# Halves of W3's row blocks between w_out's blocks, six accumulators, and another order of loads and first steps

## The chip, the cores and the metric

The kernel runs on one core of a Trainium2 chip. The metric is the device time of one execution in microseconds, the median of several runs.

## The reference

Two layers follow each other. The first is a decayed linear recurrence over q, k, v of shape 4 x 8 x 768 x 64, with one decay per head; the second is a gated product with weights:

```python
gamma = 1.0 - 2.0 ** (-5.0 - np.arange(H))
for t in range(S):
    state = gamma[None, :, None, None] * state + np.einsum('bhd,bhe->bhde', k[:, :, t], v[:, :, t])
    y[:, :, t] = scale * np.einsum('bhd,bhde->bhe', q[:, :, t], state)
x = y.transpose(0, 2, 1, 3).reshape(B * S, H * D)      # 3072 x 512
a = x @ w1                                             # w1, w2: 512 x 1024
b = x @ w2
h = a * b @ w3                                         # w3: 1024 x 1024
out = h @ w_out                                        # w_out: 1024 x 512
```

Inputs and output are float32.

## The kernel before

The products run in float16 with float32 sums. `h @ w_out` is folded ahead: the kernel computes W3O = W3 @ w_out once, as eight row blocks `W3O[f]` of 128 x 512, so that each step needs only three products: with W1, with W2 and with W3O.

The recurrence is worked in chunks of 128 rows. A step of the second layer takes 256 rows (two batches, one chunk), and there are 12 of them. The first 256 rows of batches 0 and 1 are steps 0 and 1 and are worked by the class `Pairs` (`b0` for batch 0, `b1` for batch 1); later steps by `scores`, `intra`, `kv`, `inter` and `outputs_back`. For a `Pairs` object the sequence is: cast q, k and v to float16 (`q_cast`, `k_cast`; `v_cast` multiplies by decays), transpose q and k on TensorE (PE) and copy the transposes out of PSUM, `scores` (q times k) and two masking products on VectorE (DVE) called `am_back`, twice; `intra` (scores times v), twice; `kv` and `state` (the state after 128 rows); `inter` (q times that state); `outputs_back`, twice, which scales the result on DVE into the tile `XT` that the second layer reads. `next_state_add` (DVE) and `next_state_decay` (GpSimd, POOL) prepare the state for the chunk after.

The schedule is written by hand: each engine executes its instructions in the order of the code, and the code orders PE, DVE, ScalarE (ACT), POOL and the load queue on SyncE (SP) by where each call stands. Buffers are rotated in pools. Every load goes through `dma_in`, on SP, into a stage tile of 512 KB (`new_stage`), of which there are 22; the first 22 loads need no free buffer, later ones wait until an earlier tile has been cast.

The order of loads before: W3 rows 0 to 3 alternate with the four blocks of w_out, then W3 rows 4 to 7, then q, k, v of batch 0, q, k, v of batch 1, W1 (4 tiles), W2 (4 tiles), then q, k, v of later steps. W3 and w_out have rows of 4 KB per partition; q and k, v of the first steps come in pieces of 512 bytes.

W3O is built like this. `cast_w3(f)` casts a row block to float16 (DVE and ACT, half each, for f < 4; whole on one of them after). `w3_transpose(f)` transposes it by eight PE instructions into PSUM, and DVE copies it out. `w3_part(f, i)` adds two matmuls with w_out's block i to the accumulator of f. Blocks 0 to 3 have an accumulator in PSUM each and are worked as w_out's blocks come; blocks 4 to 7 follow one at a time through `W3Block`. `busy(m)` issues m matmuls of zeros that nothing reads. `cast_wo(i)` casts w_out's block i, half on ACT and half on POOL.

After that, step 0's first product is worked by rows of W1: `by_rows(W1, ps, d)` issues eight matmuls with W1's tile d into four PSUM banks, so that it can start before all of W1 has landed. Batch 1's `scores`, `intra`, `kv` and `inter` stand between these rows. Then come `f1.a_unit(f)`, step 1's products with W1 (four matmuls each, which read all of XT[1]), then `by_rows(W2, ps, d)` between further `a_unit`s, and from there the regular steps. The tail of the W1 part (lines 818 to 825) reads:

```python
    by_rows(W1, ps, 2)
    nc.gpsimd.tensor_copy(W2[0][:, :], w2_st[0][:, :])
    nc.gpsimd.tensor_copy(W2[1][:, :], w2_st[1][:, :])
    by_rows(W1, ps, 3)
    for i in range(4):
        cast_to(pa[i], ps[i], i > 1)
    for f, tag in ((0, "X0"), (1, "Y1"), (2, "Y0"), (3, "X1")):
        f1.a_unit(f, tag)
```

In the profile PE's products with a step's x are psF (lines 636 and 795) or psG (the first `a_unit`s), psO is the product with W3O, psW the products of W3 with w_out, psA `scores`, psY `intra` and `inter`, psK `kv`.

Of the kernel before, what the change touches and what calls it, by code (L numbers as in the profile page):

```python
# [9 lines left out]
FP = mybir.dt.float32  # L10
# [8 lines left out]
def kernel(  # L19
# [51 lines left out]
    def load_q(n):  # L71

        g, e = divmod(n, 2)
        if g >= NSTEP // 2:
            return
        bp, cp = divmod(g, NCH // 2)
        q_in[n] = load_pairs(q, bp * 2 + e, cp)

    def load_pairs(src, b, cp):
        t = new_stage()  # L80
        dma_in(
            t[:, :].rearrange("p (h x) -> p h x", x=2 * D),
            src[b, :, cp * 2 * C : (cp + 1) * 2 * C, :].rearrange("h (p t) d -> p h (t d)", t=2),
        )
        return t
# [19 lines left out]
    def new_stage():  # L105
        return wstage.tile([128, 1024], FP, tag="wst", name="stg")

    def load_rows(src, i):
        t = new_stage()
        dma_in(t[:, :], src[i * 128 : (i + 1) * 128, :])  # L110
        return t

    def load_wo(i):
        t = new_stage()
        dma_in(
            t[:, :].rearrange("p (t n) -> p t n", t=2),
            moe_w_out[i * 256 : (i + 1) * 256, :].rearrange("(p t) n -> p t n", t=2),
        )
        return t

    w3_st, wo_st = [], []
    for i in range(4):
        w3_st.append(load_rows(moe_w3, i))
        wo_st.append(load_wo(i))
    for f in range(4, 8):
        w3_st.append(load_rows(moe_w3, f))
    for e in range(2):
        load_q(e)
        k_in[e] = load_pairs(k, e, 0)
        v_in[e] = load_pairs(v, e, 0)  # L130
    w1_st = [load_rows(moe_w1, d) for d in range(4)]
    w2_st = [load_rows(moe_w2, d) for d in range(4)]
    load_q(2)
    load_q(3)
# [35 lines left out]
    keep = const.tile([128, L], FP, name="keep")  # L170
    keep_t = const.tile([128, 2, 128], FP, name="keep_t")

    def masks_and_decays():

        nc.gpsimd.memset(keep[:, :], 1.0)
        for s in range(2):
            r = slice(s * L, (s + 1) * L)
            nc.gpsimd.affine_select(
                out=keep[r, :], in_=keep[r, :], compare_op=mybir.AluOpType.is_ge, fill=0.0,
                base=0, pattern=[[1, 2], [2, 32]], channel_multiplier=-1,  # L180
            )

        nc.gpsimd.memset(keep_t[:, :, :], 1.0)
        for s in range(2):
            for t in range(2):
                nc.gpsimd.affine_select(
                    out=keep_t[half(s), t, :], in_=keep_t[half(s), t, :], compare_op=mybir.AluOpType.is_ge,
                    fill=0.0, base=-t, pattern=[[1, 2], [2, 64]], channel_multiplier=-2,
                )
        for h in range(H):  # L190
            for s in range(2):
                nc.gpsimd.memset(LGP[half((h + s) % 2), s, h // 2 : h // 2 + 1], math.log(gam[h]))
        for h in range(H):
            p, r = h // 2, (h % 2) * 64
            nc.gpsimd.memset(GS[r : r + 64, p : p + 1], gam[h] ** C)
# [20 lines left out]
    def cast_to(dst, src, on_dve):  # L216
        if on_dve:
            nc.vector.tensor_copy(dst, src)
        else:
            nc.scalar.copy(dst, src)  # L220

    def cast_wo(i):
        dst = WO[i][:, :, :].rearrange("p a n -> p (a n)")
        nc.scalar.copy(dst[:, 0:512], wo_st[i][:, 0:512])  # L224
        nc.gpsimd.tensor_copy(dst[:, 512:1024], wo_st[i][:, 512:1024])  # L225

    def cast_w3(f):
        t = att.tile([128, 1024], HP, tag="qT", name="w3h", bufs=5)
        st = w3_st[f]
        if f < 4:  # L230
            nc.vector.tensor_copy(t[:, 0:512], st[:, 0:512])  # L231
            nc.scalar.copy(t[:, 512:1024], st[:, 512:1024])
        else:
            cast_to(t[:, :], st[:, :], f == 4)
        W3h[f] = t

    def bank(tag, shape, dtype, name):
        return ps_at.tile(shape, dtype, tag=tag, name=name)

    def w3_transpose(f):  # L240
        src, ps = W3h.pop(f), bank(("X0", "X1")[f % 2], [128, 1024], HP, "psW3")
        for g in range(8):
            c0 = (g // 2) * 256 + g % 2
            nc.tensor.transpose(  # L244
                ps[:, g * 128 : (g + 1) * 128], src[:, c0 : c0 + 255 : 2], ident16[:, :]
            )
        w3t[f] = att.tile([128, 1024], HP, tag="k16" if f < 3 else "v16", name="w3t", bufs=3)
        nc.vector.tensor_copy(w3t[f][:, :], ps[:, :])  # L248

    def w3_part(f, *parts):  # L250

        for i in parts:
            for r in range(2):
                g = i * 2 + r
                nc.tensor.matmul(  # L255
                    acc[f], lhsT=w3t[f][:, g * 128 : (g + 1) * 128], rhs=WO[i][:, r, :],
                    start=(g == 0), stop=(g == 7),
                )
            if i == 3:
                cast_to(W3O[f][:, :], acc[f], f < 3)  # L260

    class W3Block:
        def __init__(self, f):
# [413 lines left out]
    def cast_w(W, st, d, on_dve):  # L677
        cast_to(W[d][:, :], st[d][:, :], on_dve)

    def busy(m, tag="Y0", n=512):  # L680
        if tag:
            ps = bank(tag, [128, 512], FP, "psZ")
        else:
            ps = ps_f.tile([128, 512], FP, tag="psF", name="psZ")
        for _ in range(m):
            nc.tensor.matmul(ps[:, 0:n], lhsT=Z[:, 0:128], rhs=Z[:, 0:n], start=True, stop=True)  # L686

    cast_w3(0)
    busy(8)
    acc = [ps_f.tile([128, DM], FP, tag="psF", name="psW")[:, :] for _ in range(4)]  # L690
    w3_transpose(0)
    cast_wo(0)
    busy(2, n=400)
    w3_part(0, 0)
    busy(3)
    cast_w3(1)
    w3_transpose(1)
    busy(3)
    cast_wo(1)
    w3_part(0, 1)  # L700
    w3_part(1, 0, 1)
    cast_w3(2)
    w3_transpose(2)
    busy(2, n=400)
    cast_wo(2)
    w3_part(0, 2)
    w3_part(1, 2)
    w3_part(2, 0)
    cast_w3(3)
    w3_transpose(3)  # L710
    w3_part(2, 1, 2)
    cast_wo(3)
    masks_and_decays()
    cast_w3(4)
    for f in range(3):
        w3_part(f, 3)
    cast_w3(5)
    w3_part(3, 0, 1)
    w3_transpose(4)
    cast_w3(6)  # L720
    w3_part(3, 2, 3)
    w3_transpose(5)
    cast_w3(7)
    output_decays()
    wb = W3Block(4)
    wb.mm(4)
    w3_transpose(6)
    wb.mm(4)
    wb.back()
    q_cast(0, nc.gpsimd)  # L730
    wb = W3Block(5)
    wb.mm(4)
    w3_transpose(7)
    wb.mm(4)
    wb.back()
    b0, b1 = Pairs(0), Pairs(1)
    b0.k_cast(nc.vector)
    q_transposes(0, "Y0", False)
    b0.v_cast(nc.gpsimd, 0)
    b0.v_cast(nc.gpsimd, 1)  # L740
    wb = W3Block(6)
    wb.mm(4)
    b0.k_transposes("Y1", True)
    wb.mm(4)
    am_back = b0.scores(0)
    wb.back()
    am_back(0)
    am_back(1)
    wb = W3Block(7)
    wb.mm(3)  # L750
    am_back = b0.scores(1)
    am_back(0)
    b0.kv(True)
    b0.state()
    am_back(1)
    b0.intra(0)
    q_cast(1, nc.scalar, nc.gpsimd)
    wb.mm(1)
    q_transposes(1, "X0", False)
    b1.k_cast(nc.gpsimd)  # L760
    last = ended(b0.intra(1), nc.gpsimd)
    b0.outputs_back(0)
    wb.mm(1)
    b1.k_transposes(None, False, 2)
    b0.inter(last)
    b0.next_state_add()
    b0.outputs_back(1)
    b1.v_cast(nc.gpsimd, 0)
    nc.scalar.copy(W1[0][:, 0:512], w1_st[0][:, 0:512])  # L769
    nc.gpsimd.tensor_copy(W1[0][:, 512:1024], w1_st[0][:, 512:1024])  # L770
    b1.v_cast(nc.gpsimd, 1)
    wb.mm(1)
    am_back = b1.scores(0)
    am_back(0)
    am_back(1)
    wb.mm(2)
    wb.back()
    nc.scalar.copy(W1[1][:, 0:512], w1_st[1][:, 0:512])
    nc.gpsimd.tensor_copy(W1[1][:, 512:1024], w1_st[1][:, 512:1024])
    b0.next_state_decay()  # L780
    nc.gpsimd.tensor_copy(W1[2][:, :], w1_st[2][:, :])
    nc.scalar.copy(W1[3][:, 0:512], w1_st[3][:, 0:512])
    nc.gpsimd.tensor_copy(W1[3][:, 512:1024], w1_st[3][:, 512:1024])

    ffn = [Ffn(m) for m in range(NSTEP)]
    f0, f1 = ffn[0], ffn[1]
# [12 lines left out]

    pa = [hold[i // 2][:, i % 2 * 512 : i % 2 * 512 + 512].rearrange("p (a n) -> p a n", a=2) for i in range(4)]  # L800
    ps = four_banks()
    by_rows(W1, ps, 0, (2, 3, 4, 5))
    am_back = b1.scores(1)
    am_back(0)
    am_back(1)
    b1.intra(0)
    by_rows(W1, ps, 0, (6, 7, 0, 1))
    by_rows(W1, ps, 1, range(4))
    b1.intra(1)
    b1.kv(False)  # L810
    b1.state()
    b1.outputs_back(0)
    by_rows(W1, ps, 1, range(4, 8))
    b1.inter()
    b1.outputs_back(1)
    b1.next_state_add()
    b1.next_state_decay()
    by_rows(W1, ps, 2)
    nc.gpsimd.tensor_copy(W2[0][:, :], w2_st[0][:, :])
    nc.gpsimd.tensor_copy(W2[1][:, :], w2_st[1][:, :])  # L820
    by_rows(W1, ps, 3)
    for i in range(4):
        cast_to(pa[i], ps[i], i > 1)
    for f, tag in ((0, "X0"), (1, "Y1"), (2, "Y0"), (3, "X1")):
# [153 lines left out]
```

## Time and profile before

| | |
|---|---|
| runs, us | 183.87, 183.89, 182.86; median 183.87 |
| profiled execution | 184.97 us, of which the span in the profile is 183.3 |
| granted TensorE clock | 1.0 |
| PE busy | 174.3 us, 95% of the span, 2634 matmuls |
| DVE, ACT, POOL busy | 108.7, 71.8 and 71.5 us |
| bytes moved by DMA | 39.71 MB, mean 217 GB/s |

PE means the matmuls and PEld the loads of their stationary operand, which lie beside them. Busy shares are means over the span. The profile gives three more things that matter here: slices of the span with a digit for each engine's busy share in tenths; the chain of work that ended last, followed back from the end; and for each load its issue on SP and the time from issue to landing.

### The profile page before, as it was taken

How to read it: one execution, taken by the hardware profiler on the slowest of the kernel's cores; microseconds unless marked ns; L12 is line 12 of the kernel's file. 1: busy time of each engine (PE TensorE's matmuls, PEld its weight loads, DVE VectorE, ACT ScalarE, POOL GpSimd, SP SyncE). 2: the span in 40 equal slices, each digit the busy share in tenths (PEclk: the TensorE clock that was granted, in tenths of full speed). 3: DMA queues.
4: the chain of work that ended last, by engine and by line, in shares of the span. 5: the costliest groups of instructions: out<-in, count | busy, mean ns of one | idle time of the engine just before them, and what ended most of it. 6: DMA issues, size and time to landing. Idle time of an engine off the chain costs nothing.

```text
span 183.3 us, 6222 instructions
## 1 busy us (share of the span) xinstructions
PE 174.3 (95%) x2634; PEld 124.7 (68%) x2634; DVE 108.7 (59%) x204; ACT 71.8 (39%) x157; POOL 71.5 (39%) x127
## 2 busy tenths in 40 slices
PE   7689999799999999999999999999999999999992
PEld 2345646588766696785876858758678587685871
DVE  2247658670769678648468484395685865845430
ACT  4353844455630332433333424334244242342531
POOL 3127526864547650824416364037450260000000
PEclk9999999999999999999999999999999999999999
DMA  5999999999999989999999999999999930200203
GB/s 215 344 418 404 299 273 288 368 401 278 215 260 234 174 254 221 221 283 223 213 212 175 322 192 239 207 191 290 225 149 250 159 114 7 114 0 29 89 0 114
DMA packets 79530, 39.71 MB, mean 217 GB/s; under 512 B 57360, under 2 KB 74000, under 8 KB 79504
## 3 DMA queue, kind: packets, MB, share of 16 engines
q1 hardware_dynamic: 79072, 38.81, 89.9%
q8 instruction: 20, 0.33, 0.8%
q10 hardware_dynamic: 432, 0.52, 0.8%
q14 instruction: 6, 0.05, 0.1%
HBM read 29.36 MB, written 6.29 MB: 195 GB/s over the span
## 4 chain that ended last, share of the span: by engine, by line
PE 78%; SPq 9%; DMA 9%; ACT 1%; issue 1%; ACTq 0%
PE psF L636 40%; PE psO L663 23%; SPq L63 9%; DMA stg<-in_moe_w_out_dram 5%; DMA stg<-in_moe_w_dram 4%; PE psF L795 4%; PE psY L531 2%; PE psY L599 2%; PE psA L383 2%; PE psG L636 2%; PE psK L551 1%; PE psTk L357 1%; ACT w L220 1%; PE psTq L328 0%; ACT osb L667 0%
## 5 line engine op out<-in xcount | busy, mean ns | idle before, releaser
L636 PE MATMUL psF<-xt,w 128*128 128x256 f16 x672 | 76.5, 273 | 0.0
L636 PEld LDWEIGHTS <-w 128*128 128x128 f16 x704 | 68.4, 98 | 10.3
L651 DVE TENSOR_TENSOR ht<-pa,psF 128x256 f16<-128x256 f32 x88 | 36.9, 420 | 37.6 <-PE psF L636 31.6
L663 PE MATMUL psO<-w3o,ht 128*128 128x512 f16 (+2 forms) x200 | 44.0, 371 | 0.3 <-issue 0.3
L645 ACT COPY pa<-psF 128x256 f32<-128x256 f32 x80 | 29.7, 371 | 37.1 <-PE psF L636 37.1
L663 PEld LDWEIGHTS <-ht 128*128 128x128 f16 x200 | 18.5, 98 | 19.9 <-issue 0.6
L667 ACT ACTIVATE osb<-psO 128x512 f32<-128x512 f32 (+2 forms) x25 | 14.5, 580 | 44.4 <-PE psO L663 44.4
L614 DVE TENSOR_TENSOR xt<-psY,YS 64x512 f16<-64x512 f32 (+1 forms) x29 | 21.1, 728 | 5.2 <-PE psY L599 4.8
L310 POOL TENSOR_TENSOR v<-stg,VS 128x512 f16<-128x512 f32 x20 | 20.6, 1042 | 5.1 <-DMA stg<-in_v_dram 5.0
L303 POOL CAST k<-stg 128x512 f16<-128x512 f32 x18 | 11.0, 612 | 25.3 <-DMA stg<-in_k_dram 25.1
L290 POOL CAST q<-stg 128x1024 f16<-128x1024 f32 (+1 forms) x12 | 12.0, 1003 | 15.3 <-DMA stg<-in_q_dram 10.8
L390 DVE TENSOR_TENSOR am<-psA,keep 128x512 f16<-128x512 f32 x20 | 12.8, 680 | 0.6 <-PE psA L383 0.6
L566 POOL TENSOR_TENSOR t<-s,GS 128x512 f16<-128x512 f32 x8 | 8.3, 1040 | 12.3 <-DVE s L565 12.3
L795 PE MATMUL psF<-xt,w 128*128 128x256 f16 x64 | 8.3, 273 | 1.1 <-ACT w L769 1.0
L255 PE MATMUL psW<-wo,w3t 128*128 128x512 f16 x32 | 7.7, 379 | 1.0 <-ACT wo L224 1.0
L269 PE MATMUL psW<-wo,w3t 128*128 128x512 f16 x32 | 8.6, 381 | 0.0
L248 DVE COPY w3t<-psW 128x1024 f16<-128x1024 f16 x8 | 5.5, 688 | 4.9 <-PE psW L244 4.9
L795 PEld LDWEIGHTS <-w 128*128 128x128 f16 x64 | 5.9, 98 | 2.7 <-ACT w L769 1.5
L686 PE MATMUL psZ<-zeros 128*128 128x512 f16 (+1 forms) x18 | 5.9, 461 | 1.3 <-DVE zeros L143 1.3
L244 PEld LDWEIGHTS <-w3h 128*128 128x128 f16 x64 | 4.1, 98 | 3.7 <-DVE w3h L231 2.3
L573 DVE TENSOR_TENSOR t<-psK,t 128x512 f16<-128x512 f32 x9 | 6.2, 690 | 0.6 <-PE psK L551 0.5
L225 POOL CAST wo<-stg 128x512 f16<-128x512 f32 x4 | 2.4, 612 | 10.2 <-DMA stg<-in_moe_w_out_dram 10.2
(92 smaller groups left out, 148.1 us busy)
## 6 DMA issues: line engine op xcount, KB each, us to landing
stg<-in_moe_w_dram SPq DMA_DIRECT2D x16, 512.0 KB, 9.3
stg<-in_q_dram SPq DMA_DIRECT2D x12, 512.0 KB, 6.3
out_dram<-osb SPq DMA_DIRECT2D x22, 256.0 KB, 3.5
stg<-in_k_dram SPq DMA_DIRECT2D x20, 256.0 KB, 5.7
stg<-in_v_dram SPq DMA_DIRECT2D x20, 256.0 KB, 5.8
stg<-in_moe_w_out_dram SPq DMA_DIRECT2D x4, 512.0 KB, 7.8
stg<-in_k_dram SPq DMA_DIRECT2D x2, 512.0 KB, 10.5
stg<-in_v_dram SPq DMA_DIRECT2D x2, 512.0 KB, 8.8
```

The lines of the kernel that those rows point to most:

```text
L63: nc.sync.dma_start(dst, src)
L290: (nc.scalar.copy if eng is nc.scalar else eng.tensor_copy)(dst[:, :].rearrange("i (t h d) -> i h t d", t=2, d=D)[:, hs, :, :], src[:, :]. ...
L303: (nc.scalar.copy if eng is nc.scalar else eng.tensor_copy)(dst, src)
L310: eng.tensor_tensor(v16[:, e, :].rearrange("j (h d) -> j h d", d=D), v32[:, e, :].rearrange("j (h d) -> j h d", d=D), VS[:, 2, :].unsqueez ...
L390: nc.vector.tensor_tensor(am[:, r, :, :], ps[r][:, :, :], keep[:, :].unsqueeze(1).broadcast_to((128, NP * 2, L)), MULT,)
L614: nc.vector.tensor_tensor(XT[m][to, :, s, :].rearrange("p (a e) (i t) -> p a e t i", e=2, t=2), psYs[m][s][fr, :, :].rearrange("p (a e) (t ...
L636: nc.tensor.matmul(ps[:, :], lhsT=W[d][:, f * 128 : (f + 1) * 128], rhs=self.x(d), start=(d == 0), stop=(d == 3),)
L645: nc.scalar.copy(self.pa[f][:, :], ps[:, :])
L651: nc.vector.tensor_tensor(self.HT[:, f, :], self.pa.pop(f)[:, :], ps[:, :], MULT)
L663: nc.tensor.matmul(psO[:, :], lhsT=self.HT[:, f, e * 128 : (e + 1) * 128], rhs=W3O[f][:, cs], start=(f == 0), stop=(f == 7),)
L667: nc.scalar.activation(osb[:, cs], psO[:, :], AF.Copy, scale=final_scale)
L795: nc.tensor.matmul(ps[f // 2][:, f % 2, :], lhsT=W[d][:, f * 128 : (f + 1) * 128], rhs=f0.x(d), start=(d == 0 and f % 2 == 0), stop=(d == ...
```

## The change

The loads come in another order. W3's row blocks 0 to 5 are loaded as two halves of 512 columns each (`load_w3(f, h)`, 128 rows of 2 KB), first halves first, between w_out's blocks; rows 6 and 7 stay whole. q, k and v of batch 0 stand between the last W3 loads. Two tiles of W1 come before q, k, v of batch 1 and two after.

W3 is worked in these halves: `cast_w3(f, h)` casts 512 columns on DVE, `w3_half(f, h)` transposes them by four PE instructions and DVE copies them out. Six row blocks have an accumulator each (`acc_of`): two in the banks Y0 and Y1, four in the psF pool. Rows 6 and 7 go through `W3Block` as before. The filler matmuls write into the accumulators ahead of their first product and are shorter. The masks and the decays on POOL are made in two functions at two places.

The first two steps are ordered anew: batch 0's work follows its loads between the last W3 blocks; all of `by_rows` row 0 and half of row 1 come before batch 1's transposes and scores, row 2 lies around `intra(0)`, row 3 before `inter`. Batch 1's k cast and its two copies of transposes move to DVE; W1 row 2 is cast by ACT alone.

```diff
+    for x in ((0, 0), "o0", (1, 0), (2, 0), (3, 0), "o1", (4, 0), (5, 0),
+              (0, 1), "o2", (1, 1), (2, 1), "o3", (3, 1)):
+        if x[0] == "o":
+            wo_st[int(x[1])] = load_wo(int(x[1]))
+        else:
+            load_w3(*x)
+    load_q(0)
+    load_w3(4, 1)
+    load_w3(5, 1)
+    k_in[0] = load_pairs(k, 0, 0)
+    w3_st[6] = load_rows(moe_w3, 6)
+    v_in[0] = load_pairs(v, 0, 0)
+    w3_st[7] = load_rows(moe_w3, 7)
+    w1_st = [load_rows(moe_w1, d) for d in range(2)]
+    load_q(1)
+    k_in[1] = load_pairs(k, 1, 0)
+    v_in[1] = load_pairs(v, 1, 0)
+    w1_st += [load_rows(moe_w1, d) for d in range(2, 4)]
...
+    def cast_w3(f, h):
+        W3h[f, h] = att.tile([128, 1024], HP, tag="qT", name="w3h", bufs=5)
+        nc.vector.tensor_copy(W3h[f, h][:, 0:512], w3_st[f][:, h * 512 : h * 512 + 512])
...
+    def w3_half(f, h):
+        src = W3h.pop((f, h))
+        ps = bank(("X0", "X1")[len(units) % 2], [128, 512], HP, "psW3")
+        units.append(f)
+        for g in range(4):
...
+        nc.vector.tensor_copy(w3t[f][:, h * 512 : h * 512 + 512], ps[:, :])
...
+    def acc_of(f):
+        if f not in acc:
+            acc[f] = bank(f"Y{f}", [128, DM], FP, "psW") if f < 2 else ps_f.tile([128, DM], FP, tag="psF", name="psW")
+        return acc[f]
...
+    b0.kv(True)
+    b0.state()
+    w3_transpose(7, "X0", False)
     last = ended(b0.intra(1), nc.gpsimd)
     b0.outputs_back(0)
+    wb = W3Block(7)
+    wb.mm(2)
     b0.inter(last)
     b0.next_state_add()
     b0.outputs_back(1)
...
+    cast_w1_halves(0, nc.scalar, nc.gpsimd)
+    cast_w1_halves(1, nc.scalar, nc.gpsimd)
+    wb.mm(6)
+    wb.back()
+    q_cast(1, nc.scalar, nc.gpsimd)
+    b1.k_cast(nc.vector)
     b1.v_cast(nc.gpsimd, 0)
     b1.v_cast(nc.gpsimd, 1)
...
-    by_rows(W1, ps, 0, (2, 3, 4, 5))
+    by_rows(W1, ps, 0)
+    by_rows(W1, ps, 1, range(4))
+    q_transposes(1, "X0", True)
+    by_rows(W1, ps, 1, range(4, 8))
+    b1.k_transposes("X1", True)
+    am_back = b1.scores(0)
+    am_back(0)
+    am_back(1)
     am_back = b1.scores(1)
     am_back(0)
     am_back(1)
+    b0.next_state_decay()
+    cast_w1_halves(2, nc.scalar, nc.scalar)
+    cast_w1_halves(3, nc.scalar, nc.gpsimd)
+    by_rows(W1, ps, 2, range(4))
     b1.intra(0)
-    by_rows(W1, ps, 0, (6, 7, 0, 1))
-    by_rows(W1, ps, 1, range(4))
+    by_rows(W1, ps, 2, range(4, 8))
     b1.intra(1)
     b1.kv(False)
     b1.state()
     b1.outputs_back(0)
-    by_rows(W1, ps, 1, range(4, 8))
+    by_rows(W1, ps, 3)
     b1.inter()
     b1.outputs_back(1)
     b1.next_state_add()
     b1.next_state_decay()
-    by_rows(W1, ps, 2)
     nc.gpsimd.tensor_copy(W2[0][:, :], w2_st[0][:, :])
     nc.gpsimd.tensor_copy(W2[1][:, :], w2_st[1][:, :])
-    by_rows(W1, ps, 3)
```

`cast_w1_halves(d, *engs)` casts the two halves of W1's tile d on the two engines named.

## The prediction

> **What bounds the kernel now.** I read the page's slices first, then the chain of waits in order of time, then stretches of the head, then POOL's and DVE's instructions there.
>
> ```profile
> PE   7689999799999999999999999999999999999992
> DMA  5999999999999989999999999999999930200203
> ...
> PE psF L636 40%; PE psO L663 23%; SPq L63 9%; DMA stg<-in_moe_w_out_dram 5%; DMA stg<-in_moe_w_dram 4%; PE psF L795 4%; PE psY L531 2%; PE psY L599 2%; PE psA L383 2%; PE psG L636 2%; PE psK L551 1%; PE psTk L357 1%; ACT w L220 1%; PE psTq L328 0%; ACT osb L667 0%
> ```
>
> A slice is 4.6 us. From the eighth on TensorE is full; the only stretch where it is not is the head, and there the transfers are full from the second slice. The chain says the same: queue and transfers carry it to 33.3 us, TensorE from then on.
>
> ```profile
> 25.98 7.30 DMA stg<-in_moe_w_dram
> 33.28 0.02 issue
> 33.31 0.63 ACT w L769
> 33.93 0.05 issue
> 33.98 0.61 PE psF L795 x4
> ...
> 37.52 0.39 PE psY L498 x8
> 37.91 1.85 PE psF L795 x16
> 39.76 1.75 PE psG L636 x16
> 41.51 0.87 PE psF L795 x8
> 42.38 0.45 PE psG L636 x4
> ...
> 43.23 0.95 ACT w L220
> 44.18 0.05 issue
> 44.23 1.05 PE psF L795 x8
> ```
>
> Columns: start, length, what. The first W1 row block lands at 33.28; 5.8 us of unbroken PE work follow; step 1's first unit, `f1.a_unit(0)` (psG), starts at 39.76. From there the work is the same in both kernels and PE waits only at 44.2, so **the start of that unit fixes the end of the kernel**. I call it U. In the stretch 34 to 39.5 us PE has no gap:
>
> ```profile
> 34.00:39.50 5.50, 5.50 (x120) 4.19 (x121) 3.27 (x6) 1.96 (x4) 4.08 (x6) 1.00 1.02 408
> ```
>
> (length; busy PE, PEld, DVE, ACT, POOL; clock; DMA share; GB/s.) Between `b1.inter` (L498, over at 37.9) and U lie 16 matmuls of `by_rows` rows 2 and 3, 1.85 us. They cover the second `outputs_back` on DVE, on which U waits, and the state's sum and decay:
>
> ```profile
> 37.36 1.34 DVE L509 TENSOR_TENSOR xt<-psY,YS 128x512 f16<-128x512 f32 x2
> 38.60 0.40 DVE L483 TENSOR_TENSOR s<-psK,t 128x256 f32<-128x256 f32 x1
> ...
> 39.09 0.61 POOL L490 TENSOR_TENSOR t<-s,GS 128x256 f16<-128x256 f32 x1 [1.18 <-DVE s L483]
> 39.64 1.04 POOL L819 CAST w<-stg 128x1024 f16<-128x1024 f32 x1
> ```
>
> XT[1] is ready at 38.70, a microsecond before its use, and the first W2 block is cast by 40.68, before its use at 41.51.
>
> [...] share 1.0 from 6.6 us on, so an order of loads moves landings against each other but not the last one. [...] packets of 4 KB took 159 ns in the median, of 2 KB (the stores) 84, of 512 B 27 to 31.
>
> **Landings, the clock of the head.** From each issue and its time to landing: W3 rows 0 to 3 and w_out at 4.1, 5.4, 7.9, 9.2, 10.6, 11.8, 13.1, 14.4; W3 row 4 at 15.7; q0 21.35, k0 24.2, v0 26.1, q1 27.8, k1 29.6, v1 31.25; W1 at 33.3, 34.6, 35.9 (worked out), 37.25. A 4 KB-row tile costs 1.29 us, a q/k/v tile 1.6 to 2.9. A load is issued once the load eight places before it has landed (ninth issue at 4.68 after a landing at 4.1); with halves the eight are smaller, but the smallest eight-load window holds 5 tiles, 6.4 us of transfer, so I take no starvation.
>
> **The change, part by part.**
>
> 1. *Halves.* 12 half loads in place of 6: 6 tiles move as 2 KB packets. 16 x 84 ns against 8 x 159 per tile and engine: +0.07 us each, **+0.43 us** for every landing behind them. Bounds: -1.2 (the 2.6 us that the third load took after the second, where 1.3 is the rule, doesn't recur) to +1.2 (a W1 tile behind a q/k/v tile took 2.03, not 1.29: +0.74 for more changes of kind).
> 2. *Order.* W1 rows 0 and 1 now come before q1, k1, v1; rows 2 and 3 after. 22 tiles lie up to the last W1 row in both, so W1 row 2 lands at 35.9 + 0.43 = 36.3 and row 3 at 37.7. But v1 has two more weight tiles ahead: 31.25 + 2 x 1.29 + 0.43 = **34.3**, k1 29.6 + 3.0 = 32.6. v0 gets one tile fewer: 25.25; W3 row 7 about 26.6 (before: 19.6).
> 3. *W3 work in halves.* The transposes (64) and products (64) stay; 12 copies of 512 columns replace 6 of 1024 (0.69 us). 18 filler matmuls (5.9 us busy) become 19 of 256 columns. All of it lies ahead of 26.6 us, under the loads: counted **nothing**. Without that cover each half would cost one more DVE cast and copy with its hand-over, 6 x 0.5 us. Masks and decays on POOL are divided, same instructions, under the same cover. SP issues six loads more, 0.44 us each; a half takes 0.64 us to transfer, so SP stays ahead of the transfers.
> 4. *Tail of W3 and b0.* Row 7: ACT cast 26.6 + 1.05 = 27.7; transposes wait for `b0.kv`, which needs both v casts (25.25 + 2 x 1.04 = 27.35): 27.75 to 28.4; ACT copy 1.01 to 29.5; two products, `inter`, six products (0.215 each) to 31.7; ACT's `W3O[7]` copy to 32.35. q1's ACT cast is queued behind it: 0.62 to 33.0, though q1 landed at 30.8. Meanwhile `by_rows` 0 and half of 1: PE at 33.1.
> 5. *Batch 1's scores.* q transposes to 33.55, DVE copy to 34.5, rest of row 1, k transposes, DVE copy to 35.4, `scores(0)` 0.4, then four mask products on DVE of 0.65 to **38.6**. Batch 1's k cast comes from POOL to DVE (0.69, from 32.6, before q's copy needs DVE) and both copies from ACT to DVE, which has nothing else between 33.3 and 34.
> 6. *Rows 2 and 3 after the scores.* W1 row 2 is cast at 36.3 + 0.65 = 37.0, scores end at 37.5; four matmuls 0.5, `intra(0)` 0.45, four 0.5: 38.95. The v casts that it reads end on POOL at 34.3 + 2.08 = 36.4; batch 0's decay (0.61, moved behind them) ends at 37.0, before W1 row 3 lands, whose second half is queued behind it. So `intra(1)` starts about 38.6 to 38.95 by either road; 0.55, `kv` 0.3, row 3 (landed and cast by 38.4) 0.9, `inter` 0.39: 40.8. On the cheaper readings (rows at 0.44 per four, no scores wait) 40.5. I take 40.7.
> 7. *The cover is gone.* Nothing follows `inter` now but U. `outputs_back(1)`, 0.67 + 0.1 for the hand-over, lies open: **U at 41.5, against 39.76: +1.75.** What is late next: the sum 0.40, decay 0.61 and W2 cast 1.04 follow on DVE and POOL, so W2 row 0 is ready at 43.5 while U's four units end at 43.25: **+0.3**. The ACT cast that PE waited for at 44.2 hangs on the fifth unit, which moves along, so nothing is recovered. W2 lands by 42.9, q2 by 44.7, before their uses.
>
> Sum: 1.75 + 0.3 = **+2.05 us**. It is made against the profiled execution, 184.97 with a span of 183.3; the shown median is 183.87, 1.1 below it. I put the sum on the median: **185.9 us**, +1.1%.
>
> **Rivals.**
> - *Loads earlier* (0.20). The early 1.3 us loss doesn't recur and the whole clock moves by up to -1.2 + 0.43: U at 40.7 or a little earlier, +0.5 to +1.4, 184.4 to 185.3. For: it is one gap in a regular series. Against: the engines were full in it (share 1.00), only the packets were slower.
> - *Loads later* (0.17). Mixed tiles cost 2.0 instead of 1.29 at three or more new changes of kind, or eight small loads fall behind: W1 row 2 at 37.5, U at 42.7, +3.2, 187.1. Speaks for it: share over 1.1 but 292 GB/s around 18 to 24 us. Against: the same tiles, so gaps may just be shared out.
> - *Faster* (0.06). The W3 halves free PE early, and U follows the last W1 row alone: landing + 0.62 + 0.9 matmuls. It decides only if v1 lands by about 32, so that batch 1 is done by then; with row 3 at 36.4 (loads 1.3 ahead) U is at 38.0, -1.75, 182.1. Against: item 7's order puts `inter` behind row 3 in any case, and no byte is saved.
> - *It does nothing*: a gap in PE later swallows the delay. Speaks against it that PE waits after 44.2 sum to 0.6 us and are sequencer issue. Its share lies in the first rival's.
>
> **Numbers.** The likeliest case (0.57) holds 185.2 to 186.6 by itself. The range takes in both load rivals: **184.4 to 187.2**. This kernel's runs spread by 0.6%, so about 1% (1.84 us) is what can be told from no change. The sum lies just beyond it. Of the likeliest case two thirds (0.38) and of the late loads all (0.17) are slower by more, rounded 0.56; the rest of both the first and the likeliest, 0.38, within; 0.06 faster.
>
> **What would show it.** v1 landing at 34.3 and W1 row 2 at 36.3; q1's ACT cast starting well after its landing; in the chain, DVE `xt` (outputs_back) between `inter` and psG, with PE idle 0.7 us; psG's first unit at 41.5; `by_rows` of W2 waiting for POOL; from there the same spacing to the end. I am wrong if U is at or before 39.8, or if the distance from U to the end differs by more than half a microsecond.

## The result, and the profile after

| | before | after |
|---|---|---|
| runs, us | 182.86 to 184.07, median 183.88 | 192.65 to 196.36, median 194.1 |
| ratio | | 1.0542 (1.0466 to 1.0617) |
| profiled execution, and its span | 184.97, 183.3 | 196.36, 194.6 |
| U, the first `f1.a_unit` | 39.76 | 51.63 |
| from U to the end of the span | 143.5 | 143.0 |

The change costs 10.2 us, and all of it lies ahead of U: the rest takes nearly the same time in both. The prediction had 185.9 and U at 41.5. The profiled execution is the longest of the four and has the lowest mean clock, 0.963, where the other three have 0.982, 0.982 and 0.991; the ratio leaves it out (by the ratio the change costs 10.0 us), and what the clock does in it is told apart from the waits below.

The slices of the page after (4.9 us each; tenths of PE busy, tenths of the granted clock, tenths of DMA):

```profile
PE   7697869869899999999999999999999999999993
PEclk9969996995899999999999999999999999999999
DMA  5999999999999907979988799999999990110202
```

Before, the clock line was 9 throughout and PE full from the ninth slice on; the eighth has a 7, and slices 4 to 7 (13.7 to 32.1 us), which lie in the head, already had a 9 each. Now PE is full from the twelfth, and the clock falls to 6 in the third and seventh slices, to 5 in the tenth and 8 in the eleventh. Slices 3, 7 and 10 look full of PE work for that very reason: the same matmuls take longer (a pair of products with w_out 0.59 us from 8.55, and 1.06 from 9.95). The transfers are full in the same place as before, so the loads do not show a gap.

The same in figures, PE alone in two stretches of the head, before and after (length; PE busy and matmuls; clock; DMA share; GB/s):

```profile
8.40:24.00 15.60, 15.00 (x116) 1.00 1.07 369
24.00:34.00 10.00, 8.59 (x161) 1.00 0.99 288
```

```profile
8.40:24.00 15.60, 13.51 (x84) 0.89 1.08 363
24.00:34.00 10.00, 7.51 (x76) 0.83 1.02 302
```

Before, PE was already busy for 15.0 of 15.6 us while W3 came in; 1.3 us of that were filler (the matmuls of zeros), none of it after 12.2 us. After, PE does 84 matmuls there instead of 116. All engines from the start to U (busy PE, PEld, DVE, ACT, POOL; clock; DMA share; GB/s), before and after:

```profile
0.00:39.76 39.76, 34.84 (x420) 19.77 (x421) 21.87 (x41) 19.08 (x31) 19.07 (x69) 1.00 0.98 333
```

```profile
0.00:51.63 51.63, 40.83 (x419) 22.45 (x420) 27.15 (x52) 16.86 (x29) 17.71 (x66) 0.87 0.99 312
```

The number of matmuls is the same. Taking the filler's own busy time (same view, the filler's line alone) out of PE's gives an account of U, into which three experiments are put already:

| up to U | U | filler | other PE work | PE idle | clock |
|---|---|---|---|---|---|
| before | 39.76 | 5.91 | 28.93 | 4.92 | 1.00 |
| after | 51.63 | 4.92 | 35.91 | 10.80 | 0.87 |
| `e1_cast_ahead` | 45.20 | 4.62 | 29.72 | 10.86 | 1.00 |
| `x2_second_only` | 44.37 | 6.08 | 29.08 | 9.21 | 1.00 |
| `e3_fill` | 46.60 | 12.85 | 28.94 | 4.81 | 1.00 |

The profiled execution loses 11.87 us up to U: 5.9 of more idle time, 7.0 of the same work taking longer at a lower clock, less 1.0 of shorter filler. Two causes, then; that the second follows from the first is what the next lines and `e3_fill` below speak for. Stretches of 2 us in the kernel after, same columns:

```profile
26.00:28.00 2.00, 1.08 (x11) 0.56 (x10) 0.69 (x1) 1.28 (x3) 0.87 (x1) 1.00 1.06 341
28.00:30.00 2.00, 0.94 (x24) 0.81 (x24) 0.69 (x1) 1.17 (x2) 0.00 (x0) 1.00 1.15 293
30.00:32.00 2.00, 2.00 (x20) 0.61 (x16) 1.29 (x2) 0.00 (x0) 0.00 (x0) 0.53 1.03 260
...
42.00:44.00 2.00, 0.65 (x22) 0.53 (x25) 1.49 (x3) 0.00 (x0) 0.00 (x0) 0.94 1.14 295
44.00:46.00 2.00, 2.00 (x24) 1.08 (x23) 1.61 (x3) 0.00 (x0) 0.00 (x0) 0.50 1.16 251
46.00:48.00 2.00, 2.00 (x47) 1.30 (x51) 0.00 (x0) 0.00 (x0) 0.00 (x0) 0.50 0.96 191
```

In the head the clock is 0.50 from 9.62 to 13.04, 30.10 to 33.52 and 43.75 to 50.58 us, for 3.41, 3.41 and 6.83 us, or four times 3.41 us. In the 3.41 us just ahead of each of the three falls PE was busy for 1.77, 1.43 and 1.65 us, about half of the time. The four runs line up by it: 192.65 at a mean clock of 0.991, 193.89 and 194.32 at 0.982, 196.36 at 0.963. One stretch of 3.41 us lowers the mean clock of such a span by 0.5 x 3.41 / 194.6 = 0.009, so one, two, two and four of them are estimated from these clocks, about 1.2 us each. Without any, the kernel would take about 191.4 (an estimate from these four), so the waits are worth some 7.5 of the 10.2 us of the median, and the clock some 2.7.

What PE waits for, by the waits of the kernel after (total us, times, longest):

```profile
PE psW L269 <- DVE w3h L248: 3.4, 5, 0.9
...
PE psW L280 <- ACT w3h L255: 1.2, 1, 1.2
PE psG L679 <- DVE xt L552: 0.8, 1, 0.8
PE psA L472 <- DVE kT L237: 0.8, 1, 0.8
PE psA L472 <- DVE w3t L237: 0.8, 1, 0.8
PE psA L472 <- DVE am L479: 0.8, 1, 0.8
PE psW L312 <- ACT w3t L239: 0.8, 1, 0.8
```

The first is PE waiting for the casts of the halves, the second for row 6's cast on ACT; the rest are single hand-overs in the second part. How a half is handed over, on DVE's timeline of the kernel after (start, length):

```profile
6.58 0.43 DVE L248 CAST w3h<-stg 128x512 f16<-128x512 f32 x1 [1.43 <-DMA stg<-in_moe_w_dram]
7.50 0.42 DVE L274 COPY w3t<-psW 128x512 f16<-128x512 f16 x1 [0.49 <-PE psW L269]
7.84 0.42 DVE L248 CAST w3h<-stg 128x512 f16<-128x512 f32 x1
8.75 0.42 DVE L274 COPY w3t<-psW 128x512 f16<-128x512 f16 x1 [0.49 <-PE psW L269]
9.09 0.42 DVE L248 CAST w3h<-stg 128x512 f16<-128x512 f32 x1
```

Cast, PE's four transposes, copy, and only then the next cast: 1.25 us a half in these lines, though a half takes 0.65 us to transfer. DVE waits for PE and PE for DVE, and this twelve times for the six row blocks instead of six.

### The profile page after: what moved, and what is told of

Read it like the earlier page. It is cut to its first block, busy times and chain, and to the rows that moved or that the text cites. A ratio compares the mean times of both kernels' runs of the same rounds, so it can differ in the third digit from the quotient of the medians.

```text
span 194.6 us, 6242 instructions
## 1 busy us (share of the span) xinstructions
PE 180.5 (93%) x2635; PEld 127.4 (65%) x2635; DVE 114.3 (59%) x216; ACT 69.1 (36%) x155; POOL 70.1 (36%) x126
## 4 chain that ended last, share of the span: by engine, by line
PE 70%; issue 11%; DMA 10%; POOL 5%; SPq 2%; ACT 1%; ACTq 0%; POOLq 0%
PE psF L679 38%; PE psO L706 22%; DMA stg<-in_moe_w_dram 6%; DMA stg<-in_v_dram 4%; POOL v L458 2%; SPq L63 2%; PE psY L574 2%; PE psY L642 2%; PE psA L426 2%; PE psF L837 2%; PE psK L594 1%; PE psTk L400 1%; POOL w L816 1%; PE psG L679 1%; POOL w L870 1%
## 5 line engine op out<-in xcount | busy, mean ns | idle before, releaser
L679 PE MATMUL psF<-xt,w 128*128 128x256 f16 x672 | 76.5, 273 | 0.0
L688 ACT COPY pa<-psF 128x256 f32<-128x256 f32 x80 | 29.7, 372 | 37.1 <-PE psF L679 37.1
L298 PE MATMUL psW<-wo,w3t 128*128 128x512 f16 x48 | 14.1, 416 | 0.7 <-DVE w3t L274 0.3
L837 PE MATMUL psF<-xt,w 128*128 128x256 f16 x64 | 10.4, 308 | 0.2
L274 DVE COPY w3t<-psW 128x512 f16<-128x512 f16 x12 | 5.0, 424 | 9.4 <-PE psW L269 9.4
L269 PE MATMUL psW<-ident,w3h 128*128 128x128 f16 x48 | 5.0, 235 | 3.5 <-DVE w3h L248 3.4
L298 PEld LDWEIGHTS <-w3t 128*128 128x128 f16 x48 | 4.6, 107 | 5.3 <-issue 1.3
L269 PEld LDWEIGHTS <-w3h 128*128 128x128 f16 x48 | 3.2, 103 | 7.2 <-DVE w3h L248 6.7
L248 DVE CAST w3h<-stg 128x512 f16<-128x512 f32 x12 | 5.7, 480 | 2.3 <-DMA stg<-in_moe_w_dram 2.3
```

The costliest lines, as they stand in the source:

```text
L298: nc.tensor.matmul(acc_of(f)[:, :], lhsT=w3t[f][:, g * 128 : (g + 1) * 128], rhs=WO[i][:, r, :], start=(g == 0), stop=(g == 7),)
L679: nc.tensor.matmul(ps[:, :], lhsT=W[d][:, f * 128 : (f + 1) * 128], rhs=self.x(d), start=(d == 0), stop=(d == 3),)
L688: nc.scalar.copy(self.pa[f][:, :], ps[:, :])
L837: nc.tensor.matmul(ps[f // 2][:, f % 2, :], lhsT=W[d][:, f * 128 : (f + 1) * 128], rhs=f0.x(d), start=(d == 0 and f % 2 == 0), stop=(d == ...
```

## The experiments

Two theories at first: the **waits** (the hand-over of halves, and the order of the second part) set U by themselves; or the **clock** does, and PE kept busy would bring the time back. Medians are given with the ratio to the kernel before and its interval; U is from the profiled run.

**Three single repairs, and all three at once.** `e1_cast_ahead` issues each half's cast one half earlier:

```diff
+    cast_w3(1, 0)
     w3_half(0, 0)
...
-    cast_w3(1, 0)
     w3_part(0, 0)
+    cast_w3(2, 0)
     w3_half(1, 0)
```

> Every half's cast stands one half earlier in DVE's order, so that it no longer waits behind the copy of the half before; nothing else is changed. Serial-chain theory (DVE and PE hand each half to and fro, 1.25 to 1.8 us per half, against 0.65 us of transfer): the last w3_half ends 3 to 4 us earlier than the 25.4 us of the changed kernel, and 2 to 4 us of the 10.2 come back: 190 to 192 us. Clock theory (the loss is TensorE at half clock after idle stretches): the waits of PE grow shorter only a little, half-clock windows stay, under 1 us comes back: 193 to 194.5. Loads theory: no change, 194.

Measured: 190.67, 1.038 (1.0321 to 1.0438), U at 45.2 in a run at full clock. 3.4 us back, 3.0 by the ratios. The wait for `w3h` is gone, but its waits then read:

```profile
PE psW L298 <- DVE w3t L274: 4.2, 6, 2.0
...
PE psW L280 <- ACT w3h L255: 1.2, 1, 1.2
```

PE's idle time up to U is as long as in the kernel after (10.86 against 10.80): the cast ahead of the first copy waits itself for the second load, and the first copy stands behind it. What came back in this run is the clock: the same work took 29.7 us instead of 35.9. So the time fell in the range of the first theory without the reason that it gave.

`e2_k_pool` puts batch 1's k cast back on POOL, since on DVE it took 3.26 us in the kernel after, where the prediction had 0.69:

```diff
-    b1.k_cast(nc.vector)
+    b1.k_cast(nc.gpsimd)
```

> Only batch 1's k cast goes back from DVE to POOL. [...] the k cast is ready near 38.5 instead of 41.1, scores(0) starts about 2 us earlier, 1.5 to 2.5 us come back: 191.6 to 192.6. If the slow cast is hidden behind something else that is as late (POOL's v casts, which now start 1 us later): within 0.7 of 194.1.

Measured: 192.62, 1.0468 (1.0368 to 1.0569), U at 46.8. That is 1.5 us less than the kernel after, within the two intervals: not told apart. The cast's times on DVE in four traces stand below, under what was not expected.

`e3_fill` adds 63 filler matmuls of 256 columns where PE idles, and changes nothing else:

```diff
+    fill(5, X())
     w3_half(1, 0)
...
+    fill(10, "X0")
     w3_transpose(6, "X0", True)
+    fill(6, "X1")
...
+    fill(8, "Y0")
     am_back = b1.scores(1)
```

> Some sixty matmuls of zeros are added where PE waits (before halves' transposes, before both scores of batch 1), nothing else is changed; they compute nothing that is read. Clock theory: no window at half clock is left (granted clock 1.0), and all that PE did at half speed, some 3.5 us a window with two to three windows, of which about half lay on the path, comes back: 189 to 191. Serial-chain theory: the clock rises too, but the halves still take 1.25 us each, and only 1 to 2.5 us come back: 191.6 to 193.

Measured: 192.31, 1.0474 (1.0417 to 1.0532), clock 0.989 to 1.0. The account above shows it: 12.9 us of filler, idle time down to 4.8, other work back at 28.9 us, and U still at 46.6. The fillers took the place of the idle time, and the time came down by 1.8 us only, which is within the two intervals. So **the clock alone is not the loss**: with PE at full speed U is still at 46.6 here and at 45.2 in `e1_cast_ahead`. How much the fillers themselves delay the work behind them is not told apart.

`e4_all` does the three at once and puts row 3 behind `inter`, so that `outputs_back(1)` is covered again. Four causes are set against the loads here: hand-over, clock, k cast and cover.

```diff
-    by_rows(W1, ps, 3)
     b1.inter()
+    by_rows(W1, ps, 3)
```

> The three edits together, and row 3 of W1 after inter again, so that it covers the second outputs_back. [...] the first unit of step 1 starts at 41 to 42 us, where the landings alone allow it, and the kernel takes 185 to 187.5. If the loads or the order of batch 1 after v1 are a separate loss of several us: 189 or more.

Measured: 194.44, 1.06 (1.054 to 1.0659), U at 49.4. A clear miss. With the casts ahead there is less idle time for 63 fillers, 9.9 us of them in this run; that they stand in front of work that is ready is argued from this, not shown by a run of its own.

**The two parts apart.** `x1_halves_only` has W3 in halves with six accumulators and the shorter filler, and the order of before from row 6 on, loads included. `x2_second_only` has W3 in whole rows as before, and the new order of everything after.

```diff
     load_w3(4, 1)
     load_w3(5, 1)
-    k_in[0] = load_pairs(k, 0, 0)
-    w3_st[6] = load_rows(moe_w3, 6)
...
+    for f in range(6, 8):
+        w3_st[f] = load_rows(moe_w3, f)
+    for e in range(2):
+        load_q(e)
...
+    w1_st = [load_rows(moe_w1, d) for d in range(4)]
```

> The first half of the change alone: W3 rows 0 to 5 in halves, six accumulators, short fillers, the changed order of those loads; from W3 row 6 on loads and program of the kernel before. Hand-over theory (PE was full from 8.4 us on before, so every wait that the halves put between DVE and PE delays the end): 3 to 5 us slower than before, the first unit of step 1 at 43 to 45 us, and half-clock windows in some runs. Second-part theory (the loss comes from the new order of batches 0 and 1 against W3's last rows and W1): within 1 us of before.

```diff
-    for x in ((0, 0), "o0", (1, 0), (2, 0), (3, 0), "o1", (4, 0), (5, 0),
-              (0, 1), "o2", (1, 1), (2, 1), "o3", (3, 1)):
...
+    for i in range(4):
+        w3_st.append(load_rows(moe_w3, i))
+        wo_st.append(load_wo(i))
+    for f in range(4, 6):
+        w3_st.append(load_rows(moe_w3, f))
     load_q(0)
-    load_w3(4, 1)
-    load_w3(5, 1)
```

> The second half of the change alone: W3 rows 0 to 5 whole and with the fillers of before, then the changed kernel's loads and program from W3 row 6 on. Hand-over theory: most of the loss is gone; what is left is the open outputs_back, batch 1's late v, the k cast on DVE and the row of waits around batch 0's scores: 2 to 4 us slower than before. Second-part theory: 6 us or more slower. The prediction's own sum, which counted only this part, gives 2.

Measured: 187.76, 1.0243 (1.0168 to 1.0318), U at 42.4; and 190.12, 1.0356 (1.0289 to 1.0423), U at 44.4. Against 183.43 beside them, +4.3 and +6.7 us; together 11.0, the whole loss of 10.2 within the intervals. Each part alone costs what the theory that blamed it had said, so neither theory has the whole. The first part keeps the waits of the halves (PE's waits, as above):

```profile
PE psW L266 <- DVE w3h L245: 3.4, 5, 0.9
PE psW L277 <- ACT w3h L252: 1.6, 2, 0.8
```

The second part runs at full clock in its profile, so its delay can be read step by step. PE there, from 27 us:

```profile
27.93 0.88 PE L441 MATMUL psA<-qT,kT 64*64 64x128 f16 x16
28.75 1.04 PE L281 MATMUL psW<-wo,w3t 128*128 128x512 f16 x4
29.71 0.42 PE L462 MATMUL psY<-am,v 64*64 64x128 f16 x16
29.96 0.42 PE L479 MATMUL psK<-v,k 64*64 64x64 f16 x32
30.32 0.62 PE L256 MATMUL psW<-ident,w3h 128*128 128x128 f16 x8
30.87 0.42 PE L462 MATMUL psY<-am,v 64*64 64x128 f16 x16
32.04 0.61 PE L281 MATMUL psW<-wo,w3t 128*128 128x512 f16 x2 [0.76 <-ACT w3t L225]
```

Row 7's transposes (`ident`, 30.32) stand behind batch 0's `scores(1)`, row 6's products, `intra(0)` and `kv`. They start 2.6 us later than the 27.75 of the prediction, and everything after keeps that: batch 1's q transposes at 35.72 (33.1), its masks done at 40.93 (38.6), U at 44.37 (41.5).

**Repairs in the parts.** `x4_row7_early_cover` is the second part with row 7's transposes ahead of `scores(1)` and row 3 behind `inter`; `x5_halves_ahead` the first part with the casts ahead, all but the first; `e5_ahead_pool` the whole change with those casts and the k cast on POOL.

```diff
+    w3_transpose(7, "Y0", False)
     am_back = b0.scores(1)
...
-    w3_transpose(7, "X0", False)
...
-    by_rows(W1, ps, 3)
     b1.inter()
+    by_rows(W1, ps, 3)
```

> The second half of the change alone, with two of its places moved: the transposes of W3 row 7 stand before the second scores of batch 0 (in the bank Y0, free by then) instead of behind intra(0) and kv, and W1 row 3 stands behind inter again. Queue theory (row 7 and all behind it wait for batch 0's scores, masks and kv in PE's own order, which the prediction left out): PE's waits of 0.76 for row 7's copy and of 0.82 for outputs_back go and the first unit of step 1 moves from 44.4 to 42 to 43, 187.5 to 188.7 us. If v of batch 1, which lands at 34, sets the end whatever stands before it: within 0.7 of 190.1.

> The first half of the change alone (halves), with every half's cast but the first issued one half earlier on DVE. Hand-over theory: most of the 4.3 us of the halves comes back, 184.5 to 186. If the halves cost by their smaller loads or their extra instructions instead: 187 to 188.

> The changed kernel with every half's cast one half earlier on DVE, except the first (which in the earlier experiment held up the first copy for 2.5 us until the next load landed), and batch 1's k cast on POOL. Hand-over theory: the first unit of step 1 moves from 45.2 to 42 to 43.5 us, 187 to 189 us. If the first copy was hidden behind the next load anyway: as the earlier experiment, 190 to 191.

Measured: 187.99, 1.0211 (1.0144 to 1.0277), U at 44.3 in a profiled run with a mean clock of 0.982 (0.82 from 34 to 42 us), 2.1 less than `x2_second_only`, with PE's waits for row 7's copy and for `outputs_back` gone; 186.07, 1.0124 (1.0077 to 1.0171), U at 41.9, 1.7 less than `x1_halves_only`; 189.92, 1.0355 (1.027 to 1.044), U at 46.3, 4.2 less than the change (3.4 by the ratios). The order of the halves' casts is a cause, worth about 1.7 us, and so are row 7's and row 3's places, about 2 us for both together. Neither part comes back to the time before: of the first, 2.4 us are left, and whether they come from the waits that remain (2.1 us for copies of halves, 1.6 for casts on ACT), the shorter filler or the smaller loads was not tested. `e5_ahead_pool` missed the 187 to 189 of its first theory.

`x6_batch1_before_w1` is the second part with batch 1 loaded and worked ahead of W1, as in the kernel before; `z2_batch1_casts` adds to it batch 1's k cast on POOL and its q cast ahead of ACT's `W3O[7]` copy.

```diff
-    w1_st = [load_rows(moe_w1, d) for d in range(2)]
     load_q(1)
     k_in[1] = load_pairs(k, 1, 0)
     v_in[1] = load_pairs(v, 1, 0)
-    w1_st += [load_rows(moe_w1, d) for d in range(2, 4)]
+    w1_st = [load_rows(moe_w1, d) for d in range(4)]
...
-    by_rows(W1, ps, 0)
-    by_rows(W1, ps, 1, range(4))
...
     cast_w1_halves(3, nc.scalar, nc.gpsimd)
-    by_rows(W1, ps, 2, range(4))
+    by_rows(W1, ps, 0)
     b1.intra(0)
```

> The second half of the change alone, but with q, k, v of batch 1 loaded before all of W1, as in the kernel before, and batch 1's transposes and scores before row 0 of W1; rows 2 and 3 follow inter. Batch-0 queue theory: W3's last block still ends near 34 us, some 1.5 us later than before, and 2 to 3.5 us remain: 185.5 to 187. Load-order theory (v of batch 1 behind two tiles of W1): nearly all is back, under 185. If neither: 188 or more.

```diff
-    wb.back()
     q_cast(1, nc.scalar, nc.gpsimd)
-    b1.k_cast(nc.vector)
+    wb.back()
+    b1.k_cast(nc.gpsimd)
```

> The miss of the experiment with batch 1 loaded before W1, with batch 1's k cast on POOL and its q cast on ACT ahead of W3's last copy. If the miss came from these two casts (2.70 us on DVE beside POOL's v casts; 1.2 us of PE waiting for q) and the half clock that the waits brought: 186 to 188 with a granted clock near 1.0. If batch 0's queue alone had set it: 190 to 191.6.

Measured: 191.59, 1.0438 (1.0391 to 1.0485), clock 0.982 in every run, U at 46.9; and 187.93, 1.028 (1.0218 to 1.0343), clock 1.0 in three of four, U at 43.1. The old order of these loads, with batch 1's work moved up to fit it, brought nothing: PE waited 1.2 us for the q cast, which stood on ACT behind the copy of `W3O[7]`, k's cast took 2.70 us, and the clock was 0.76 from 36 to 38 us, 0.50 to 42 and 0.53 to 44. The two casts alone are worth 1.6% by the ratios, some 2.9 us, in waits and clock together.

**The filler, and the order of scores, in the kernel before.** `x3_before_8_fillers` leaves out 10 of the 18 filler matmuls of before, work that nothing reads, so that 8 are left; `y1_scores_before_rows` takes from the new order one thing only, batch 1's scores and `intra(0)` ahead of `by_rows` row 0, with both v casts before W1's.

```diff
-    busy(2, n=400)
...
-    busy(3)
...
-    busy(3)
...
-    busy(2, n=400)
```

```diff
-    by_rows(W1, ps, 0, (2, 3, 4, 5))
     am_back = b1.scores(1)
...
     b1.intra(0)
-    by_rows(W1, ps, 0, (6, 7, 0, 1))
+    by_rows(W1, ps, 0, (2, 3, 4, 5, 6, 7, 0, 1))
```

> The kernel before without ten of its 18 filler matmuls, those after the first eight; they compute nothing. Clock theory: with them gone PE is idle for about half of the time between 5 and 10 us, a window of 3.4 us at half clock follows in most runs, and it costs 1 to 3 us. If the fillers only fill waits: within 0.5 us, granted clock 1.0.

> The kernel before with two moves: batch 1's second v cast stands before POOL's half of W1's first cast, and the second scores and intra(0) stand before row 0 of W1, where PE waited 1.0 us for W1's first row to land. If PE's work after that landing sets the start of step 1: 0.3 to 0.6 us faster, 182.9 to 183.2. If the last row of W1 sets it instead: within 0.2.

Measured: 184.62, 1.006 (1.0035 to 1.0085), with clocks mostly from 0.978 to 0.991; and 183.51, 0.9991 (0.9969 to 1.0014). The ten fillers are worth 1.2 us. That they earn it through the clock is not shown: 15 of the 17 runs without them have a clock below 1.0, but the two at 1.0 took 184.59 and 185.1 us, no less than the others. The moved scores change nothing that can be measured.

**All that helped, together.** `z1_all_repairs` is the kernel after with the casts ahead, row 7's transposes early, the k cast on POOL and row 3 behind `inter`.

```diff
+    cast_w3(2, 0)
     w3_half(1, 0)
...
-    cast_w3(2, 0)
...
+    w3_transpose(7, "Y0", False)
     am_back = b0.scores(1)
...
-    b1.k_cast(nc.vector)
+    b1.k_cast(nc.gpsimd)
...
-    by_rows(W1, ps, 3)
     b1.inter()
+    by_rows(W1, ps, 3)
```

> The changed kernel, loads unchanged, with four repairs of order and no added filler: halves' casts one half earlier, row 7's transposes before batch 0's second scores, batch 1's k cast on POOL, W1 row 3 behind inter. If waits in the engines' own queues are the loss, the gains found singly add up (3.5 or more, 2, 1.5): 186 to 188. If the loads of the changed kernel hold the start of step 1 at 44 whatever the queues do: 188.5 or more.

Measured: 190.42, 1.0374 (1.0317 to 1.043), clocks 0.964 to 0.991, U at 45.9: a miss, and no better than `e5_ahead_pool` or `e1_cast_ahead`. Two stretches of it:

```profile
24.00:28.00 4.00, 2.02 (x30) 1.08 (x28) 1.62 (x3) 2.15 (x3) 2.04 (x2) 0.92 1.05 379
28.00:32.00 4.00, 4.00 (x44) 2.14 (x46) 2.08 (x4) 1.06 (x2) 0.00 (x0) 0.66 1.03 271
```

W3's halves are done earlier, and PE then waits for row 6's cast (1.20 us) and copy (0.78). It is busy for 2.0 of 4.0 us, and the mean clock is 0.66 in the stretch that follows, and 0.62 again from 40 to 44 us. The gains of single repairs did not add up: what one wait gave back was lost at the next, with time at half clock on top. No version tried beats the kernel before; `y1_scores_before_rows` equals it.

## Why the prediction was wrong

- **That U fixes the end: right in the main.** From U to the end the two kernels take 143.5 and 143.0 us. The difference is 0.57 us, just past the half microsecond that the prediction had named as a sign against it, and the kernel after is the shorter one.
- **Items 1 and 2, the landings: right where it counts.** v1 landed at 34.55 (34.3 predicted), W1 row 2 at 36.25 (36.3). W3 row 7 at 25.1 (26.6) and v0 at 23.85 (25.25) came 1.4 to 1.5 us early, a lead that was lost again by v1. The loads were not late, and their lead did not help, so neither of the load rivals holds: U moved by 12 us while the last loads before it came as foretold.
- **Item 3, "all of it lies ahead of 26.6 us, under the loads: counted nothing": the step that failed first.** The loads covered nothing, since PE was itself full there, 15.0 of 15.6 us. The first part alone costs +4.3 us, with 3.4 us of waits for the casts; moving those casts gave 1.7 of it back. The item's own uncovered price, 6 x 0.5 = 3 us, was near it. It named the price of a lost cover and did not ask PE's busy time whether there was one, though the prediction's own PE line shows a 9 in slices 4 to 7; its text reads TensorE as full only from the eighth slice on, which has a 7.
- **Item 4, row 7: mis-sized.** It held the transposes by `b0.kv` and the v casts alone, 27.75. PE's own queue ahead of `kv` (scores, masks, row 6's products, `intra(0)`) was left out: 30.32 in `x2_second_only`, +2.6, and 34.50 in the kernel after, where PE was idle from 27.1 to 28.3 for row 6's cast and ran at half clock from 30.1. ACT's copy ended at 32.0 there and 36.2 here, not at 29.5. With item 6's half microsecond this takes U in `x2_second_only` from the predicted 41.5 to 44.4.
- **Item 5, the k cast of 0.69: POOL's work beside it was not asked about.** It took 3.26 us on DVE in the kernel after, beside POOL's work, and 0.68 in `x2_second_only`. The masks were done at 45.7 and 40.9, not at 38.6.
- **Item 6: half a microsecond short.** From the masks to U it counted 2.9 us; `x2_second_only` took 3.44 at full clock, the kernel after 5.9, most of it at a clock of 0.50 (until 50.58).
- **Item 7: right, and a small part of the whole.** `outputs_back(1)` lies open for 0.82 us (0.77 predicted), in the kernel after:

```profile
51.63 1.58 PE L679 MATMUL psG<-xt,w 128*128 128x256 f16 x13 [0.82 <-DVE xt L552]
```

  Behind it POOL's decay starts at 51.97 and W2's cast at 52.52, in the order foretold; `by_rows` of W2 follows U after 1.99 us, against 1.75 before (+0.3 predicted).
- **A clock of 1.0, taken for granted: wrong.** The prediction priced every matmul at the 1.0 of before. In the profiled execution after, stretches at 0.50 made the same PE work 7.0 us longer; of the median's loss they are an estimated 2.7 us.
- **The range.** It took in mistakes of the loads, up to +3.2 us, and none of the compute queues. The rival that was missing is the one in which the new order makes PE, DVE and ACT wait for each other. That the kernel is slower came out as foretold, but most of the loss came through steps that the prediction had counted as nothing.

What stays open: how much of the 10.2 us is each wait's alone, since each wait, and each stretch at a clock of 0.50, moves the waits behind it; and what the 4.2 us of `e5_ahead_pool` are made of, since the k cast by itself (`e2_k_pool`) could not be told from no gain. One wait was left in every version of the whole change without added filler, PE's 1.20 us for row 6's cast: its load had landed by 22.1 us in the kernel after, but on ACT the cast stands behind the copy of `W3O[5]`, which starts at 27.12. No experiment moved it.

## What to carry to other kernels

Before work is counted as hidden under the loads, read the busy time of the engine that does it in that very stretch: full transfers cover nothing for an engine that is full too (here PE, busy for 15.0 of 15.6 us at a DMA share of 1.07). Cutting a tile in halves doubles its hand-overs, and with cast, transpose and copy alternating between two engines each half costs a round trip, 1.25 us here against 0.65 of transfer. Where an order brings gaps to TensorE, price them as waits and read the granted clock behind them as well (here an estimated 7.5 and 2.7 us), and do not count on repairs adding up.

## What was not expected of the hardware

**A cast on DVE took 3.26 us beside POOL's work, and 0.68 in another place.** Batch 1's k cast on DVE (float32 to float16, both in SBUF) and POOL's work beside it, in the kernel after:

```profile
37.85 3.26 DVE L333 CAST k<-stg 128x1024 f16<-128x1024 f32 x1
```

```profile
37.40 2.03 POOL L458 TENSOR_TENSOR v<-stg,VS 128x512 f16<-128x512 f32 x2
39.41 0.60 POOL L533 TENSOR_TENSOR t<-s,GS 128x256 f16<-128x256 f32 x1
39.96 0.60 POOL L816 CAST w<-stg 128x512 f16<-128x512 f32 x1
```

and in `x2_second_only`, where both start in the same moment:

```profile
33.66 0.68 DVE L302 CAST k<-stg 128x1024 f16<-128x1024 f32 x1
```

```profile
33.66 2.58 POOL L427 TENSOR_TENSOR v<-stg,VS 128x512 f16<-128x512 f32 x2 [0.41 <-DMA stg<-in_v_dram]
```

In the first DVE comes second, and its cast ends 0.55 us after POOL's fourth instruction in a row. In `x6_batch1_before_w1` it is the same: 2.70 us, ended 0.55 after POOL's last. In the second the cast takes 0.68 us, and POOL's pair 2.58 where it took 2.03 in the first, 0.55 longer. `e1_cast_ahead` has the same as the second: both start at 34.5 us, 0.68 for the cast and 2.59 for the pair. So in the two traces where the cast began while POOL's instructions followed each other without a gap, it ended 0.55 us after the last of them; in the two where both began together it was over first. Why is not shown by these times.

**The clock fell after half-busy stretches, and the falls lie multiples of 3.41 us apart.** In the kernel after the clock goes to 0.50 at 9.62, 30.10 and 43.75 us, six and four times 3.41 us apart. A last fall, at 193.94 behind PE's last matmul, comes 44 times 3.41 us after the third. In `z1_all_repairs` the mean clocks of the stretches (0.92 from 24 us, 0.66 from 28, 0.62 from 40) put the falls near 27.3 and 41.0, an estimate, again four times 3.41 apart. Ahead of the three falls in the head of the kernel after PE was busy for 1.77, 1.43 and 1.65 of 3.41 us. Counted in steps of 3.41 us from 9.62, the clock of the kernel after stayed at 1.00 after steps with 2.47 us (from 16.45), 2.56 (from 23.27) and 2.65 (from 33.51). Where between 1.77 and 2.47 us the difference lies is not told by these figures. Why the runs of this one kernel have mean clocks from 0.963 to 0.991 was not tested. Nor is it told when the clock comes back: from 43.75 us in the kernel after PE was busy for 3.39 of 3.41 us and the clock stayed at 0.50 for another 3.41 us, while the step from 30.10, with PE busy throughout, was followed by 1.00.
